# Key maxima as two float32r parts made on GpSimd, value buffers by first freed, and a new order table, in a phi-attention and cosine-FFN kernel

## The chip, the cores and the metric

The kernel runs on one core of one Trainium2 chip. The metric is the device time of one execution in microseconds (us). Three runs of the kernel before gave 1011.79, 1012.16 and 1014.1 us: a median of 1012.16 us.

Engine names in the rows: PE is TensorE, DVE is VectorE, ACT is ScalarE, POOL is GpSimd, SP is SyncE, which issues nearly all DMAs.

## The reference, cut to what matters

```python
def phi(x):                                   # x: q or k, 8 x 8 heads, 576 tokens of 64
    proj = einsum('bhsd,df->bhsf', x, w_phi)  # 128 features
    proj = proj - max(abs(proj), axis=-1)     # one maximum per token
    return concatenate([exp(proj), exp(-proj)], axis=-1)
q_p, k_p = phi(q), phi(k)
kv = einsum('bhsf,bhsd->bhfd', k_p, v);  z = sum(k_p over tokens)
x = (q_p @ kv) / (q_p @ z + 1e-06)            # 4608 tokens of 512
h = x @ w_in                                  # 512 -> 2048
out = (h * cos(h)) @ w_out                    # 2048 -> 512
```

## The kernel before

**Attention.** The 64 heads are worked in 32 units of two heads. For each unit one DMA brings q and k (`qk`), another the values with a column of ones (`vs`, two buffers that units take in turn). TensorE projects q (L572, L575) and k (`k_mm`, L618, and `k_end`, L643, for the last tokens). VectorE reduces each projected key to its absolute maximum (`k_max`, L656, tile `mk`), ScalarE takes the exponentials (`exp_k`, L673 and L676), TensorE forms `kv` (`kv_mm`, L722 and L728) and then the output (`x_mm`, L755 and L761). On the side of q the maximum goes over VectorE, three small GpSimd copies (`q_spread`, L603), a VectorE transposition (`q_turn`, L607) and four GpSimd subtractions (`q_sub`, L611).

In the first seven units (`K_SUMS`) the maximum of each key is subtracted by TensorE: `k_sub` (L664) multiplies a constant matrix `minus` (-1 on its diagonal) with `mk` spread over 128 columns and adds into the PSUM bank that holds the projection. Both operands are float32, so that the program runs each such product as two matmul records. There are 14 of these steps (units 0 to 6, two banks each; the short third part and all later units give the maximum to ScalarE as a bias instead). ScalarE can then take the exponential of a whole bank in one instruction for each sign (L673).

**FFN.** Weights arrive as 64-bit words, are converted into float32r pairs (high and low part) and stored; some are summed (`fold`: loaded as `f_raw` at L508, summed at L511 and L518, stored as `wo_sums`). 9 chunks of 512 tokens follow: the first three in 9 plain visits beside the attention (first product L974, second L1023 to L1025), then the other six, two at a time, in three fast visits (`visit_two`; first product at L1201 in steps of six matmuls that the planner calls `wide`, second product at L1374 to L1376). Float32r operands are multiplied as high x high, high x low and low x high. Before each fast visit x is loaded into four `x_raw` buffers (L1116) and split; the weights of the second product go through three `wo` buffers, loaded at L1351 (from `wo_parts`) or L1347 (from `wo_sums`).

**Order.** The program is a list of 3852 steps, each with its engine, cost, dependences and buffers. `ORDER` is a table written out by hand with the number of each step in program order; `plan()` walks it and every engine gets its instructions in that order, so that an instruction that waits holds everything behind it on its engine, and a DMA that waits for a buffer holds every later DMA of the SP queue. PSUM banks go to whichever was used last the longest ago in the table; the two value buffers alternate.

Of the kernel before, what the change touches and what calls it, by code (L numbers as in the profile page):

```python
# [26 lines left out]
def phi_attention_then_cos_ffn(ctx: ExitStack, tc: tile.TileContext, qkT, vS, w_phi, w_in, w_out, out, out_t):  # L27
# [41 lines left out]
    class Step:  # L69
# [190 lines left out]
    def plan():  # L260
        place = {steps[x]: i for i, x in enumerate(ORDER)}
        owner = [None] * len(banks)
        n_v = 0

        def last(b):
            return -1 if b is None else max(place[v] for v in b.users)
# [1327 lines left out]
```

## Time and profile before

| | us |
|---|---|
| median of three runs | 1012.16 |
| profiled execution, whole time | 1013.98 |
| profiled execution, first to last instruction (span) | 1012.3 |
| PE busy, share of the span | 991.7, 98% |
| DVE busy | 892.5, 88% |
| ACT busy | 769.7, 76% |
| POOL busy | 164.3, 16% |
| DMA, mean | 208 GB/s |

An engine is busy from an instruction's start to its end; matmul ends are modelled and matmuls overlap, so the distance between the starts of two matmuls says how long one holds the engine, not its duration. The granted TensorE clock is a share of 2.4 GHz; over the whole execution it was 0.998.

### The profile page before, as it was taken

What the parts mean: (1) busy time and instruction counts of PE and PEld (TensorE: products, weight loads), DVE (VectorE), ACT (ScalarE), POOL (GpSimd) and SP (SyncE); (2) the same over time, 40 slices, a digit from 0 to 9 for tenths busy, and PEclk for the clock granted to TensorE, in tenths of its full rate; (3) what the DMA queues carried; (4) which work ended last, traced back from release to release, by engine and by line L of the source; (5) the groups of instructions that cost most, each with busy time, mean ns of one, the idle gap of its engine ahead of it and who ended that gap; (6) DMA issues with size and microseconds to landing.
All of it is one profiled execution on the core that took longest, in us unless ns stands there. A gap on an engine that the chain in (4) does not pass through costs nothing.

```text
span 1012.3 us, 22252 instructions
## 1 busy us (share of the span) xinstructions
PE 991.7 (98%) x8586; PEld 803.5 (79%) x8586; DVE 892.5 (88%) x1590; ACT 769.7 (76%) x1575; POOL 164.3 (16%) x231
## 2 busy tenths in 40 slices
PE   9999999999999999999989999899999999999997
PEld 6778878888788878788767888688888888888886
DVE  6999999999899999899989979798778998787984
ACT  6899999688878988899997666557565766665653
POOL 4544130121112123333550000000000000000000
PEclk9999999999999999999999999999999999999999
DMA  6667776456676578888767663447546575375364
GB/s 233 187 192 229 240 214 206 138 188 233 208 236 205 212 227 286 282 283 254 232 198 247 222 217 141 158 165 270 200 151 228 171 219 206 126 247 203 98 225 145
DMA packets 104569, 210.60 MB, mean 208 GB/s; under 512 B 21392, under 2 KB 52240, under 8 KB 100880
## 3 DMA queue, kind: packets, MB, share of 16 engines
q1 hardware_dynamic: 104320, 209.13, 62.4%
q8 instruction: 67, 1.10, 0.4%
q14 instruction: 38, 0.31, 0.1%
q10 hardware_dynamic: 144, 0.07, 0.0%
HBM read 152.54 MB, written 56.62 MB: 207 GB/s over the span
## 4 chain that ended last, share of the span: by engine, by line
PE 77%; DVE 10%; DMA 7%; ACT 2%; issue 2%; POOL 1%; SPq 1%; DVEq 0%; POOLq 0%; ACTq 0%
PE bank L1201 23%; PE bank L974 9%; PE bank L1374 7%; PE bank L1376 7%; PE bank L1375 7%; PE bank L1023 3%; PE bank L1025 3%; PE bank L1024 3%; PE bank L755 3%; PE bank L722 3%; PE bank L618 2%; PE bank L572 2%; DMA vs<-vS 1%; DVE mk L656 1%; DVE m L589 1%
## 5 line engine op out<-in xcount | busy, mean ns | idle before, releaser
L1374 PE MATMUL bank<-gh,wo 128*128 128x512 f32 x336 | 132.4, 394 | 6.0 <-DMA wo<-wo_parts 4.2
L676 ACT ACTIVATE ek<-bank,mk 128x128 f32<-128x128 f32 x464 | 132.9, 486 | 4.2 <-DVE mk L659 2.3
L611 POOL TENSOR_TENSOR pq<-pq,bq 128x288 f32<-128x288 f32 x128 | 120.1, 969 | 97.9 <-DVE bq L607 72.0
L1376 PE MATMUL bank<-gl,wo 128*128 128x512 f32 x336 | 132.0, 393 | 0.0
L1375 PE MATMUL bank<-gh,wo 128*128 128x512 f32 x336 | 131.7, 392 | 0.0
L682 ACT ACTIVATE eq<-pq 128x576 f32<-128x576 f32 x128 | 83.8, 793 | 6.2 <-POOL pq L611 4.8
L603 POOL COPY m<-m 32x36 f32<-32x36 f32 x96 | 43.4, 452 | 268.3 <-DVE m L598 254.2
L1298 ACT ACTIVATE g<-hs 128x512 int32<-128x512 f32 x96 | 59.6, 626 | 34.7 <-DVE hs L1217 33.6
L1304 ACT ACTIVATE g<-g,halfpi 128x512 f32<-128x512 f32 x96 | 66.9, 717 | 24.8 <-DVE g L1301 24.6
L1201 PE MATMUL bank<-x_eq,wi 128*128 128x512 f32 x216 | 84.8, 393 | 0.1
L1211 ACT ACTIVATE hs<-bank 128x512 f32<-128x512 f32 x96 | 56.0, 591 | 35.6 <-PE bank L1201 25.2
L1374 PEld LDWEIGHTS bank<-gh,wo 128*128 128x128 f32 x336 | 63.4, 189 | 21.5 <-issue 6.7
L1023 PE MATMUL bank<-wo,gh 128*128 128x512 f32 x192 | 77.2, 402 | 0.6 <-ACT pq L583 0.4
L1201 PE MATMUL bank<-xh_t,wi 128*128 128x512 f32 x192 | 76.0, 396 | 0.3 <-ACT hs L1211 0.3
L1025 PE MATMUL bank<-wo,gl 128*128 128x512 f32 x192 | 75.3, 392 | 0.3 <-DVE gl L55 0.2
L1024 PE MATMUL bank<-wo,gh 128*128 128x512 f32 x192 | 74.9, 390 | 0.0
L1376 PEld LDWEIGHTS bank<-gl,wo 128*128 128x128 f32 x336 | 63.5, 189 | 14.2
L1301 DVE SCALAR_TENSOR_TENSOR g<-g,hs 128x512 f32<-128x512 int32 x96 | 64.9, 686 | 11.1 <-ACT g L1298 10.8
L1375 PEld LDWEIGHTS bank<-gh,wo 128*128 128x128 f32 x336 | 63.6, 189 | 13.8
L755 PEld LDWEIGHTS bank<-kv,eq 128*64 128x64 f32 x2048 | 64.9, 138 | 11.8 <-issue 3.4
L755 PE MATMUL bank<-kv,eq 128*64 128x65 f32 x2048 | 70.8, 223 | 1.3 <-DVE rb L781 0.5
L722 PE MATMUL bank<-vs,ek 128*64 128x65 f32 x2048 | 67.4, 223 | 1.9 <-ACT ek L676 1.5
(170 smaller groups left out, 2517.2 us busy)
## 6 DMA issues: line engine op xcount, KB each, us to landing
wi<-wi_parts SPq DMA_DIRECT2D x18, 1792.0 KB, 7.6
wo<-wo_sums SPq DMA_DIRECT2D x20, 1024.0 KB, 6.1
qk<-qkT SPq DMA_DIRECT2D x31, 640.0 KB, 5.3
x_raw<-xs SPq DMA_DIRECT2D x47, 256.0 KB, 4.0
wo<-wo_parts SPq DMA_DIRECT2D x22, 512.0 KB, 8.8
vs<-vS SPq DMA_DIRECT2D x32, 325.0 KB, 4.9
wi_raw<-w_in SPq DMA_DIRECT2D x8, 1024.0 KB, 6.3
wo_raw<-w_out SPq DMA_DIRECT2D x8, 1024.0 KB, 6.6
```

The costliest lines, as they stand in the source:

```text
L611: qeng.tensor_tensor(out=d["pq"][:, c], in0=d["pq"][:, c], in1=d["bq"][:, c], op=ALU.subtract)
L676: ACT.activation(out=e[:, g, s * P:(s + 1) * P], in_=pk[:, g, :], func=AF.Exp, scale=1.0 - 2.0 * s, bias=d["lk" if s == 0 else "mk", i][:, ...
L722: PE.matmul(out=acc[c:c + 64, n, i, :], lhsT=e[:, s, P * n + c:P * n + c + 64], rhs=vs[b["v"].slot][:, 2 * s + i, :], start=(s == 0 and i ...
L755: PE.matmul(out=ps[64 * h:64 * h + 64, 65 * t:65 * t + 65], lhsT=d["eq", i][:, n, c:c + 64], rhs=d["kv"][:, 2 * n + i, :], start=h not in ...
L974: PE.matmul(out=bank(b), lhsT=w[:, part, 2 * r + kt // 2, kt % 2 * P:(kt % 2 + 1) * P], rhs=d.get(("from", kt), d)[x, kt], start=(k == 0), ...
L1023: PE.matmul(out=a, lhsT=gh[:, t], rhs=w[:, 0, r], start=first, stop=False)
L1024: PE.matmul(out=a, lhsT=gh[:, t], rhs=w[:, 1, r], start=False, stop=False)
L1025: PE.matmul(out=a, lhsT=gl[:, t], rhs=w[:, 0, r], start=False, stop=last)
L1201: PE.matmul(out=bank(bank_b), lhsT=w[:, part, block, j * P:(j + 1) * P], rhs=d[x, name, j], start=start and k == 0, stop=k == 5, skip_grou ...
L1374: PE.matmul(out=a, lhsT=w_of(0, m), rhs=n["gh"], start=first, stop=False, skip_group_check=True)
L1375: PE.matmul(out=a, lhsT=w_of(1, m), rhs=n["gh"], start=False, stop=False, skip_group_check=True)
L1376: PE.matmul(out=a, lhsT=w_of(0, m), rhs=n["gl"], start=False, stop=True, skip_group_check=True)
```

## The change

1. `mk` is split on GpSimd: a new step `k_split` before each of the 14 `k_sub` steps makes a float32r high part (`tensor_scalar`) and a low part (`tensor_tensor`), each of 128 partitions x 4 elements. `k_sub` then runs two float32r products in place of one float32 product. `minus` becomes float32r, made from a float32 tile by one more GpSimd instruction at the start.
2. A value buffer is chosen as PSUM banks are: the one whose last use in the table is the earliest.
3. The table is a new one of 3866 numbers (14 steps more, so every later number shifts). Counted on PE with the new steps left out, 592 of 785 steps stand at another place, by up to 24 places; on SP 370 of 411, by up to 116.

What the new table does at the places that the prediction speaks of, counted from the two tables:

- Between the place of a `k_max` and that of the `k_sub` that uses it lie 3 to 8 PE steps, 5.3 on the mean of the 14 (before 1 to 6, 3.7 on the mean); about half of them are the short `k_end`, `q_end` and `k_sub`. On POOL, up to four `q_sub` steps and a `q_spread` stand near a `k_split`.
- In the old table all `x_mm` steps come before the first `wide` step. In the new one five `wide` steps stand before the last `x_mm` (of unit 31), and the summing of the last two `wo_parts` blocks comes later.
- The weights for the last two pairs of the first fast visit (the third load at L1351, two DMAs): in the old table they are queued on SP behind an `x_raw` load whose buffer VectorE frees while PE is one step of six matmuls ahead of the first use. In the new table six such steps lie between the last of the releases (of the `wo` buffer, and of the `x_raw` buffer queued ahead) and the first use.
- The weights for the first half of the last product (L1347): four steps of six matmuls between release and first use in the old table, six in the new one.

```diff
-        0, 3, 42, 4, 5, 59, 7, 45, 44, 1, 6, 8, 9, 17, 18, 10, 19, 46, 21, 11, 48, 58, 1265, 47, 12, 62, 14, 23, 20, 22, 15, 2, 49, 25,
...
+        0, 3, 5, 44, 4, 7, 60, 6, 8, 9, 62, 10, 1, 46, 65, 48, 63, 17, 11, 19, 22, 18, 20, 64, 12, 47, 70, 61, 49, 25, 68, 66, 23, 1279,
...
-        n_v = 0
+        owner_v = [None] * len(vs)
...
                 elif b.ring == "v":
-                    b.slot, n_v = n_v, 1 - n_v
+                    b.slot = min(range(len(vs)), key=lambda i: last(owner_v[i]))
+                    assert last(owner_v[b.slot]) < place[x]
+                    owner_v[b.slot] = b
...
-    minus = const.tile([P, P], F32, name="minus")
-    POOL.memset(minus, -1.0)
-    POOL.affine_select(out=minus, in_=minus, pattern=[[-1, P]], compare_op=ALU.is_equal, fill=0.0, base=0,
+    minus = const.tile([P, P], F32R, name="minus")
+    ones = const.tile([P, P], F32, name="ones")
+    POOL.memset(ones, -1.0)
+    POOL.affine_select(out=ones, in_=ones, pattern=[[-1, P]], compare_op=ALU.is_equal, fill=0.0, base=0,
                        channel_multiplier=1)
+    hi_of(POOL, minus, ones)
...
+        def k_split(i):
+            n = NSLOT if i < 2 else 1
+            parts = d["hk", i] = new("pk" if i < 2 else "pk_t", [P, n, 2], F32R, "hk", "hpk" if i < 2 else "hpk_t")
+            hi_of(POOL, parts[:, :, 0], d["mk", i])
+            lo_of(POOL, parts[:, :, 1], d["mk", i], parts[:, :, 0])
+
         def k_sub(i):
             n = NSLOT if i < 2 else 1
             pv = d["pk", i] = d["kps", i][:, 0:P * n].rearrange("p (g f) -> p g f", f=P)
-            PE.matmul(out=pv, lhsT=minus, rhs=d["mk", i].unsqueeze(2).broadcast_to([P, n, P]), start=False, stop=True,
-                      skip_group_check=True)
+            for k in range(2):
+                PE.matmul(out=pv, lhsT=minus, rhs=d["hk", i][:, :, k].unsqueeze(2).broadcast_to([P, n, P]), start=False, stop=k == 1,
+                          skip_group_check=True)
...
-                kms[i] = Step("PE", 0.86, lambda i=i: k_sub(i), [kms[i]], use=[kb[i], pks[i]], kind="a.k_sub")
+                kms[i] = Step("POOL", 0.3, lambda i=i: k_split(i), [kms[i]], use=[pks[i]], port=True, kind="a.k_split")
+                kms[i] = Step("PE", 0.46, lambda i=i: k_sub(i), [kms[i]], use=[kb[i], pks[i]], kind="a.k_sub")
```

`hi_of` on GpSimd is `tensor_scalar(out, in, 1.0, 0.0, mult, add)`, `lo_of` is `tensor_tensor(out, in, hi, subtract)`.

## Rows read from the trace of the kernel before

**Rows 1.** Page, part 1: busy time and instructions of each engine.
```profile
PE 991.7 (98%) x8586; PEld 803.5 (79%) x8586; DVE 892.5 (88%) x1590; ACT 769.7 (76%) x1575; POOL 164.3 (16%) x231
```

**Rows 2.** Windows, busy us by stretch: span, PE, PEld, DVE, ACT, POOL, clock, DMA, GB/s.
```profile
0.00:75.00 75.00, 73.14 (x1214) 55.58 (x1216) 65.51 (x138) 60.63 (x133) 36.48 (x57) 1.00 0.64 206
75.00:400.00 325.00, 324.22 (x3159) 266.36 (x3154) 304.48 (x532) 285.43 (x584) 70.64 (x94) 1.00 0.66 216
400.00:475.00 75.00, 72.60 (x1003) 58.53 (x1003) 69.47 (x147) 67.89 (x179) 28.14 (x38) 1.00 0.82 267
475.00:540.00 65.00, 59.51 (x1229) 48.64 (x1228) 60.34 (x139) 61.22 (x175) 29.02 (x44) 1.00 0.73 225
...
630.00:645.00 15.00, 10.78 (x41) 8.31 (x40) 10.07 (x17) 8.37 (x16) 0.00 (x0) 0.89 0.52 175
645.00:990.00 345.00, 344.98 (x1499) 280.75 (x1498) 293.18 (x472) 216.03 (x376) 0.00 (x0) 1.00 0.57 190
990.00:1012.00 22.00, 16.81 (x74) 13.30 (x72) 9.46 (x15) 7.29 (x12) 0.00 (x0) 1.00 0.35 127
```

**Rows 3.** Lines by shape, L1374 and k_max: count, busy us, mean ns, idle before.
```profile
L1374 PE MATMUL bank<-gh,wo 128*128 128x512 f32 x336 | 132.4, 394 | 6.0 <-DMA wo<-wo_parts 4.2 <-DMA wo<-wo_sums 1.7
...
L656 DVE TENSOR_REDUCE mk<-bank 128x4 f32<-128x512 f32 x64 | 42.6, 672 | 0.5 <-PE bank L618 0.3
```

**Rows 4.** Chain of waits, 600 to 1012 us: start, us, what.
```profile
626.11 1.39 PE bank L1201 x6
...
633.84 6.04 DMA wo<-wo_parts
...
640.02 0.47 PE bank L1374
...
642.35 0.43 PE bank L1374
...
644.36 0.23 PE bank L1376
...
990.28 6.99 DMA wo<-wo_sums
```

**Rows 5.** Timeline of the SP queue: start, us with its wait, line, DMA.
```profile
612.26 2.49 SPq L1351 DMA_DIRECT2D wo<-wo_parts  x4
615.09 18.65 SPq L1116 DMA_DIRECT2D x_raw<-xs  x2
633.84 1.18 SPq L1351 DMA_DIRECT2D wo<-wo_parts  x2
```

**Rows 6.** The tile mk: durations of k_sub's records, ns min/median/max.
```profile
L664 PE MATMUL bank<-mk,minus x28: 592/592/697, 10.5 to 63.7; 128*128 128x512 f32 x28
```

**Rows 7.** Timeline of all engines, 42 to 44 us: start, us, engine, line.
```profile
42.39 2.21 POOL L603 COPY m<-m 32x36 f32<-32x36 f32 x3 [1.10 <-DVE m L598]
...
42.69 1.02 PE L664 MATMUL bank<-mk,minus 128*128 128x512 f32 x2
...
43.36 1.16 DVE L398 SCALAR_TENSOR_TENSOR wo_t<-wo_raw,wo_t 128x1024 uint32<-128x1024 uint32 x1
```

**Rows 8.** Chain of waits, 255 to 266 us: a stretch of L974.
```profile
259.07 5.44 PE bank L974 x24
```

**Rows 9.** Lines L603 and L611 on POOL: durations, ns min/median/max.
```profile
L603 POOL COPY m<-m x96: 206/210/2384, 9.1 to 525.4; 32x36 f32<-32x36 f32 x96
...
L611 POOL TENSOR_TENSOR pq<-pq,bq x128: 791/808/1842, 11.8 to 530.0; 128x288 f32<-128x288 f32 x128
```

**Rows 10.** DMA issues by line: count, KB each, median us to landing.
```profile
wo<-wo_sums SPq DMA_DIRECT2D x20, 1024.0 KB, 6.1
...
wo<-wo_parts SPq DMA_DIRECT2D x22, 512.0 KB, 8.8
f_raw<-wo_parts SPq DMA_DIRECT2D x8, 1024.0 KB, 6.5
```

**Rows 11.** Waits of the SP queue, value loads: us in total, times, longest.
```profile
SPq L558 <- PE bank L728: 17.1, 6, 5.5
```

335 rows, old and new, of the table ORDER are left out of this document.

## The prediction

> **What bounds the kernel now.** I read the page's busy times first [rows 1]: PE works 98% of the span, DVE 88%, ACT 76%, POOL 16%. PE is the bound, but an average hides where another engine sets the pace, so the windows come next [rows 2]. The reader is to see four kinds of stretch. From 75 to 400 us and from 645 to 990 us PE has no visible idle time (0.8 and 0.0 us): there only fewer or cheaper matmuls help. From 0 to 75 us PE idles 1.9 us, while DVE is busy 65.5 of 75. From 400 to 540 us, the last attention units, PE idles 2.4 + 5.5 us, and in the second part DVE (60.3 of 65) and ACT (61.2 of 65) are busier than PE (59.5): the units' chain over three engines sets the end there. From 630 to 645 us and after 990 us PE idles 4.2 and 5.2 us; the lines view says what ended most of that [rows 3]: DMAs into `wo`, 4.2 us of `wo_parts` and 1.7 us of `wo_sums`. The chain of waits [rows 4] shows both places, at 633.84 and 990.28 us, and the timeline of the SP queue [rows 5] why the first is late: an `x_raw` load issued from 615.09 us on waited and held SP for 18.65 us with its neighbour; the weights behind it left only at 633.84 and landed 6.04 us later. They were late by their place in the queue, not by a slow transfer.
>
> **The change part by part.** The sum is made against the profiled execution, 1013.98 us (its span of 1012.3 and 1.7 around it); the median of the runs is 1.8 us below that.
>
> *The products of `k_sub`.* One record takes 592 ns and the two of one step together 1.02 us [rows 6, 7], so the second starts 0.43 us after the first and a step holds PE for 2 x 0.43 = 0.86 us. A float32r matmul of 128x512 in L974 holds it for 5.44 / 24 = 0.227 us [rows 8]; the new step has two, 0.45 us. Removed: 14 x 0.41 = 5.7 us, all before 75 us. No row shows a float32r product with its moving operand spread from one column; the float32 one runs at the plain rate, so I take 0.227. If it ran as slowly as the old pair, a step would hold PE for 4 x 0.43 and 14 steps would cost 12 us more.
>
> *The splits.* 28 small instructions on POOL, each of 4 elements on 128 partitions. Nearest row: the copies of 32x36, median 210 ns [rows 9]; a step is then 0.42 us, 14 are 5.9 us on an engine that is busy 36.5 of the first 75 us [rows 2]. No work of POOL's is on the bound. What matters is the wait put into the chain `k_max` - `k_split` - `k_sub`: `k_max` takes 0.67 us [rows 3], the split 0.42, together 1.1 us. Between the two places in the new table stand 5.3 PE steps on the mean. A step of the first 75 us holds PE 0.9 us on the mean (73.14 us over the 82 steps there, [rows 2]), half of those in question are short ones; I call the cover about 3 us, an estimate, and some 1.7 at the tightest. So the plain split is hidden. It is not when POOL is held: the slowest copy took 2.384 us [rows 9], and the three at 42.39 took 2.21 us together while DVE ran an instruction with two SBUF inputs [rows 7]. Behind a waiting `k_split` stand the `q_sub` steps and with them ACT's exponentials of q; behind a waiting `k_sub` all of PE. Bounds: nothing, if the cover holds everywhere; 14 x (0.67 + 2.38 + 0.21 - 3) = 3.6 us, if each split meets the slowest copy. On the side below nothing, the new table has at most the 1.9 us of PE's idle time in this stretch to give back. I take +1.5, since some splits are also queued behind `q_sub` steps (808 ns each, [rows 9]) and DVE, at 65.5 of 75, becomes the next limit once PE has 5.7 us less to do. The one POOL instruction for `minus` falls into the wait for the first loads: nothing.
>
> The Trainium skill ("SBUF — State Buffer", section "Who interferes with whom") states that a DVE instruction with two SBUF inputs and a GpSimd instruction that reads SBUF lock each other out for a whole instruction. It speaks against this change, since `k_split` reads SBUF twice while DVE converts weights with two-input instructions; the slow copies at 42.39 agree. By the rule each of the 28 could wait for one; that is the third rival below.
>
> *The first blocked load.* In the new table six steps of six matmuls lie between the last release and the first use of these weights. Such a step of L1201 takes 1.39 us [rows 4], so there are 8.3 us, against 6.04 us from issue to landing; before it was one step, 1.4 us. The stall should go: 4.2 us of idle time [rows 3], and what followed it. After the stall the granted clock of the window is 0.89 [rows 2], and matmuls stand 0.43 us apart, not 0.23 [rows 4]: that is the lower of the two clock levels, after an idle PE. From 640.02 to 644.36 run 12 matmuls, 4.34 - 12 x 0.23 = 1.6 us late. Together -5.8 us. What is late next: the same kind of load takes 8.8 us at the median when issued amid others [rows 10]; then 0.5 us would remain.
>
> *The last load.* Before, four steps (5.5 us) against 6.99 us to landing [rows 4]: 1.7 us of stall [rows 3]. In the new table six steps, 8.3 us, against 6.99 or the median of 6.1 [rows 10]: gone, -1.7.
>
> *The overlap at the end of attention.* Five `wide` steps, 5 x 1.39 = 6.95 us of PE work, now stand inside the stretch where PE idles 5.5 us in 65. They need the split x earlier and four more copies from PSUM on ACT, which is itself busy 61.2 of 65. Bounds: -5.5 (all of the idle time is filled) and +3 (ACT and DVE, already fuller than PE, get the chain of the last units 5% later). I take -3. The later summing lets `f_raw` loads arrive late (6.5 us, [rows 10]) on a DVE that has more room after 540 us: nothing.
>
> *Value buffers.* The waits of value loads for `kv_mm` are at most 5.5 us each and 17.1 in all [rows 11], on SP; a better choice can only move them, and PE shows no idle time behind most: 0, with -1 to +1 as bounds.
>
> *All else in the table.* Nearly every step has another neighbour. From 75 to 400 us there is 0.8 us of idle time to win; a single new blocked transfer costs up to 5.8. I take 0 and keep -1 to +6 for the range.
>
> Sum: 1013.98 - 5.7 + 1.5 - 5.8 - 1.7 - 3 = 999.3 us against the profiled execution, 997.5 against the median. I forecast 998.5.
>
> **The rivals.** (A) The weights come in time but the front gains nothing: DVE and ACT, not PE, set the pace up to 540 us. For: their shares after 475 us, DVE's 65.5 of 75 at the start. Against: PE has almost no idle time from 75 to 400 us, so a front that starts earlier stays earlier. Time: 1013.98 - 7.5 = 1006.5.
>
> (B) `k_sub` gains, but the new table only moves the blocked transfers: another load stands behind one that waits. For: SP still has one queue, with 370 of 411 steps at other places. Against: the two known stalls get 8.3 us of cover. Time: 1013.98 - 5.7 = 1008.3.
>
> (C) Slower: GpSimd, held by DVE. Place: the 14 `k_split` in the first 75 us. Price: each of the two instructions waits for one DVE instruction of 1.16 us as at 43.36 [rows 7], so 2 x (1.16 + 0.21) = 2.7 us, with 0.67 for `k_max` and one or two `q_sub` ahead (0.8 to 1.8 us each, [rows 9]) 4.2 to 5.2 us against about 3 of cover: 1.5 us late, 14 times, 21 us. It decides from 16.2 / 14 = 1.2 us late per step, where it eats all that the other terms win (16.2 us). Time: 1013.98 - 16.2 + 21 = 1018.8. Against it: the median copy is 210 ns and only few were held.
>
> (D) More than I count: the idle time of 400 to 540 us goes wholly (7.9 us, not 3) with the rest as in the sum and no loss in front: 1013.98 - 5.7 - 5.8 - 1.7 - 7.9 = 992.9.
>
> (E) The change doesn't do what it says, as the float32r product of a spread column is as slow as the old pair: 998.5 + 5.7 + 12 = 1016.
>
> **How the numbers follow.** Forecast 48%, with its own range 994 to 1003 (the bounds of the splits, the overlap and one small new wait); A 17%, B 13%, D 10%, C 6%, E 2%; 4% for a loss elsewhere in the table that cancels the gain, near 1012. About 0.3%, 3 us, is what a measurement of this kernel can tell from no change: faster is below 1009.1 us, slower above 1015.2. Faster: the forecast, A, D and two thirds of B, 84%. Same: the rest of B, the 4% and small parts of C and E, 10%. Slower: 6%. The range 992 to 1008.5 leaves out C, E, the cancelled case and the edges of B and D.
>
> **What would show it.** Right: `k_sub` records 0.23 us apart and 28 POOL instructions near 0.2 us; PE's starts of the first fast visit some 8 us earlier; no idle time of L1374 behind `wo` DMAs; no half-clock stretch after 600 us; PE idle below 5 us between 400 and 540 us. Wrong: PE waiting for `k_split` by over 1 us a step, PE idle time over 4 us before 75 us, or a new gap behind a DMA in the fast visits.

## The result and the profile after

The changed kernel takes 1000.43 us (median of 4 runs, 999.44 to 1000.98) against 1011.97 us before (4 runs, 1010.2 to 1014.1): a ratio of 0.9884, 95% interval [0.9863, 0.9905]. That is 1.9 us above the forecast, inside the forecast's own range. The profiled execution took 1000.19 us with a span of 998.4.

Lines of the changed kernel: `k_sub` is L676, `k_split` L52 (high part) and L55 (low part), `k_max` L661, `q_sub` L616, the `mm1` products L987, the first of the fast products on `wo` L1387. The page's busy times and the windows, in the stretches and columns of [rows 1, 2]:

```profile
PE 985.3 (99%) x8586; PEld 802.2 (80%) x8586; DVE 890.4 (89%) x1590; ACT 771.7 (77%) x1575; POOL 173.3 (17%) x260
```

```profile
0.00:75.00 75.00, 73.16 (x1260) 58.61 (x1262) 64.85 (x137) 61.23 (x132) 42.43 (x86) 1.00 0.68 220
75.00:400.00 325.00, 321.83 (x3085) 262.59 (x3080) 303.44 (x525) 284.31 (x583) 73.64 (x91) 1.00 0.65 213
400.00:475.00 75.00, 74.57 (x1103) 61.84 (x1100) 71.98 (x158) 71.04 (x186) 25.09 (x39) 1.00 0.88 295
475.00:540.00 65.00, 61.23 (x1178) 49.54 (x1177) 61.68 (x138) 62.39 (x175) 32.17 (x46) 1.00 0.69 213
...
630.00:645.00 15.00, 15.00 (x67) 12.36 (x66) 14.24 (x24) 10.69 (x20) 0.00 (x0) 1.00 0.69 222
```

The reader is to see where PE's idle time went. From 630 to 645 us it was 4.2 us and is none, and the granted clock is 1.00, not 0.89. From 400 to 540 us it was 2.4 + 5.5 us and is 0.4 + 3.8. From 75 to 400 us it rose, from 0.8 to 3.2 us. In the first 75 us nothing seems to have changed: PE is as busy as before, though its subtractions now hold it for 7.65 us and not for 12.8 (28 records each, from the start of each to PE's next start). The lines by shape say the same of the loads (count, busy us, mean ns, idle time before and what ended it, against [rows 3]); the 6.0 us behind `wo` are gone:

```profile
L1387 PE MATMUL bank<-gh,wo 128*128 128x512 f32 x336 | 131.5, 391 | 0.2 <-DVE o_t L1461 0.2
```

The tile `hk` of the changed kernel, the answer to [rows 6] (ns min/median/max), has the new records, and no instruction of a split above 0.52 us. From the start of a record to the next start on PE it is 0.21 to 0.32 us, so a step holds PE for 0.55 us on the mean (forecast 0.45):

```profile
L676 PE MATMUL bank<-hk,minus x28: 379/379/483, 10.1 to 60.8; 128*128 128x512 f32 x28
L52 POOL TENSOR_SCALAR hk<-mk x14: 185/195/203, 9.5 to 58.9; 128x4 fp32r<-128x4 f32 x14
L55 POOL TENSOR_TENSOR hk<-mk,hk x14: 203/205/517, 9.8 to 59.1; 128x4 fp32r<-128x4 f32 x14
```

A single row measures the pace of the front: where the first `mm1` product starts, behind 81 PE steps before and behind the same but one (`k_end` of unit 8, 0.2 us) after. The two numbers at the end of "first and last start" belong to the products of `xh_b`; first the kernel before, then the changed one:

```profile
L974 PE MATMUL bank<-xh_b,wi x192: 387/389/526, 71.6 to 445.5; 128*128 128x512 f32 x192
```

```profile
L987 PE MATMUL bank<-xh_b,wi x192: 387/389/504, 69.7 to 444.5; 128*128 128x512 f32 x192
```

Of 5.2 us less work on PE ahead of that product (12.8 - 7.65) 1.9 us show, and by the last one 1.0. A single row of this kind is weak: two kernels below that differ only by splits whose results nobody reads start this product 2.0 us apart, the one with more work first.

### The profile page after: what moved, and what is told of

The parts are those of the page before. It is cut to its first block, busy times and chain, and to the rows that moved or that the text cites. A ratio compares the mean times of both kernels' runs of the same rounds, so it can differ in the third digit from the quotient of the medians.

```text
span 998.4 us, 22304 instructions
## 1 busy us (share of the span) xinstructions
PE 985.3 (99%) x8586; PEld 802.2 (80%) x8586; DVE 890.4 (89%) x1590; ACT 771.7 (77%) x1575; POOL 173.3 (17%) x260
## 4 chain that ended last, share of the span: by engine, by line
PE 77%; DVE 9%; ACT 7%; DMA 4%; issue 2%; SPq 1%; POOL 0%; DVEq 0%; ACTq 0%; POOLq 0%
PE bank L1214 23%; PE bank L1389 8%; PE bank L1387 8%; PE bank L1388 8%; PE bank L987 7%; PE bank L735 4%; PE bank L768 4%; PE bank L1036 3%; PE bank L1038 2%; PE bank L1037 2%; PE bank L577 2%; PE bank L623 2%; ACT ek L688 2%; DMA wi_raw<-w_in 1%; PE bank L741 1%
## 5 line engine op out<-in xcount | busy, mean ns | idle before, releaser
L616 POOL TENSOR_TENSOR pq<-pq,bq 128x288 f32<-128x288 f32 x128 | 123.4, 993 | 94.5 <-DVE bq L612 72.4
L1387 PE MATMUL bank<-gh,wo 128*128 128x512 f32 x336 | 131.5, 391 | 0.2 <-DVE o_t L1461 0.2
L688 ACT ACTIVATE ek<-bank,mk 128x128 f32<-128x128 f32 x464 | 130.1, 443 | 0.5 <-DVE mk L664 0.3
L1317 ACT ACTIVATE g<-g,halfpi 128x512 f32<-128x512 f32 x96 | 67.1, 716 | 18.6 <-DVE g L1314 18.1
L1387 PEld LDWEIGHTS bank<-gh,wo 128*128 128x128 f32 x336 | 63.0, 188 | 14.1 <-DVE o_t L1461 0.6
L1230 DVE TENSOR_TENSOR hs<-bank,hs 128x512 f32<-128x512 f32 x72 | 49.1, 686 | 25.2 <-PE bank L1214 19.5
```

The costliest lines, as they stand in the source:

```text
L616: qeng.tensor_tensor(out=d["pq"][:, c], in0=d["pq"][:, c], in1=d["bq"][:, c], op=ALU.subtract)
L688: ACT.activation(out=e[:, g, s * P:(s + 1) * P], in_=pk[:, g, :], func=AF.Exp, scale=1.0 - 2.0 * s, bias=d["lk" if s == 0 else "mk", i][:, ...
L1387: PE.matmul(out=a, lhsT=w_of(0, m), rhs=n["gh"], start=first, stop=False, skip_group_check=True)
```

## Experiments

The times of a group stand beside runs of the kernel before on the same chip: medians of 1011.78, 1011.43, 1011.31 and 1012.21 us. Ratios are against those. Differences below about 2 us between kernels of different groups are read with care. Steps are named as in the order table, with unit and part: `k_split.u2.1`.

### The change taken apart: which part gives what

**The split alone, in the old table.**

```diff
 # ORDER of the kernel before, for each part of units 0 to 6
  k_max.u0.0,
+ k_split.u0.0,
# k_sub: two float32r products, as in the changed kernel
```

> The old order table with only the new subtraction in it: each split step of GpSimd stands right behind the max step it needs, the value buffers alternate as before, nothing else is moved. Theory A (the stretch up to 75 us and the tables behind it are bound by TensorE, so shorter subtractions count in full): the kernel before less about 5 us, 1006 to 1008 us. Theory B (the pace there is set by VectorE and ScalarE, and what TensorE saves comes back as short waits): 1 to 2 us less than before, 1010 to 1011 us.

Measured: 1019.04 us (10 runs, 1016.87 to 1021.74), ratio 1.0068 [1.0044, 1.0091]. Neither theory: it is 7.3 us slower than before. GpSimd's waits in the first 75 us of its trace (us in total, times, longest) and a piece of its timeline show what changed there; the single row between the two is of the changed kernel:

```profile
POOL hk L52 <- DVE mk L664: 14.9, 5, 8.5
...
POOL pq L619 <- ACT ek L688: 4.3, 2, 2.8
```

```profile
9.51 0.20 POOL L52 TENSOR_SCALAR hk<-mk 128x4 fp32r<-128x4 f32 x1 [7.71 <-DVE mk L661]
```

```profile
58.04 1.79 POOL L611 COPY m<-m 32x36 f32<-32x36 f32 x3 [1.99 <-DVE m L606]
62.19 0.19 POOL L52 TENSOR_SCALAR hk<-mk 128x4 fp32r<-128x4 f32 x1 [2.36 <-DVE mk L664]
62.47 0.20 POOL L55 TENSOR_TENSOR hk<-mk,hk 128x4 fp32r<-128x4 f32 x1
62.62 1.57 POOL L619 TENSOR_TENSOR pq<-pq,bq 128x288 f32<-128x288 f32 x2
65.31 1.02 POOL L52 TENSOR_SCALAR hk<-mk 128x4 fp32r<-128x4 f32 x1 [1.12 <-DVE mk L664]
66.42 0.20 POOL L55 TENSOR_TENSOR hk<-mk,hk 128x4 fp32r<-128x4 f32 x1
66.57 2.00 POOL L619 TENSOR_TENSOR pq<-pq,bq 128x288 f32<-128x288 f32 x2
```

GpSimd came to the split before VectorE had the maximum, and the `q_sub` steps (L619) stood behind it. Of the 14.9 us, 8.5 are the wait for the program's first maximum, which the changed kernel has too (7.71 us); the other four waits come to 6.4 us. From 0 to 70 us PE was busy 61.59 us, against 68.14 in the same window of the kernel before, and behind that the clock fell (window 70 to 80 us of this run):

```profile
70.00:80.00 10.00, 8.80 (x128) 6.62 (x130) 7.29 (x14) 7.67 (x22) 5.70 (x6) 0.66 0.59 199
```

A mean of 0.66 between the levels 1.0 and 0.5 means 6.8 of 10 us at the lower one (1.2 GHz), at most 3.4 us of work. This trace is that of the shortest of the ten runs: their granted clock has a median of 0.9925, that of the kernel before 0.998, a difference worth at most 5.6 us of work over 1019 us. The first `mm1` product starts at 82.1 us here, not at 71.6.

**The new table without the split.**

```diff
-            for k in range(2):
-                PE.matmul(out=pv, lhsT=minus, rhs=d["hk", i][:, :, k] ...
+            PE.matmul(out=pv, lhsT=minus, rhs=d["mk", i] ...      # float32, as before
-            k_split(i)
```

> The new table and the new value buffers, but the maxima subtracted by one float32 product as before, without the split. Theory A: the changed kernel (1000.4) and about 5 us more, 1005 to 1006 us, and the subtraction steps hold TensorE 0.86 us and more again. Theory B: 1 to 2 us more, 1001.5 to 1002.5 us, because TensorE had waited for the other engines there anyway.

Measured: 1003.11 us (6 runs, 1001.96 to 1004.11), ratio 0.9915 [0.9884, 0.9947]. So the table gives 8.7 us, and the split with its products 2.7 more, near theory B; the runs of this kernel and of the changed one don't overlap, though the intervals of their ratios do. The products of `xh_b`, first and last start:

```profile
L984 PE MATMUL bank<-xh_b,wi x192: 387/389/501, 74.1 to 447.7; 128*128 128x512 f32 x192
```

The first starts 2.5 us later than before the change, so in this trace the new table by itself is the worse one for the front. With the table held, the new subtraction takes 5.5 us off PE (13.2 - 7.65); of these 4.4 are there at the first `mm1` product (74.1 to 69.7) and 3.2 at the last (447.7 to 444.5). From 75 to 400 us PE idles 2.0 us here and 3.2 in the changed kernel: part of what the front won is handed back behind it.

**The blocked load alone.**

```diff
 # SP's order in the kernel before
+ r.load2#2   (third group of wo_parts, L1351), right behind n.mm2#9
  x_raw load
- r.load2#2
```

> The kernel before with one step moved: the third load of the output weights is issued from SP's queue ahead of the x_raw load that it stood behind. Theory A (the stall at 636 to 644 us is that load's place in the queue): the 4.2 us of idle time and the 1.6 us at half clock behind it both go, 5 to 6 us less than before, 1006 to 1007 us, and the granted clock of 630 to 645 us is 1.00. Rival: the stall moves to the x_raw load or to the next load of output weights, and the time stays within 1 us of before, 1011 to 1013 us.

Measured: 1005.23 us (9 runs, 1002.93 to 1010.03), ratio 0.994 [0.9913, 0.9967]: 6.5 us less than before, theory A, 0.8 us below its range. The window 630 to 645 us and the line by shape of this run:

```profile
630.00:645.00 15.00, 15.00 (x67) 12.32 (x67) 14.72 (x25) 10.86 (x19) 0.00 (x0) 1.00 0.43 145
```

```profile
L1379 PE MATMUL bank<-gh,wo 128*128 128x512 f32 x336 | 132.3, 394 | 2.0 <-DMA wo<-wo_sums 1.9
```

The 4.2 us behind `wo_parts` and the half-clock stretch are gone together, by moving one step of one queue; the 1.9 us behind `wo_sums` at the end stay, as the last load was left where it was. Not all of the difference between the two traces is this load: after 300 of the 2016 matmuls of the fast visits this kernel is 4.0 us ahead already (PE idles 0.1 us from 400 to 475 us, not 2.4, with the same steps there), after 600 it is 10.1 us ahead. The load's own part in the traces is 6.1 us.

**The overlap taken back.**

```diff
 # ORDER of the changed kernel, behind the last attention product
- n.wide#0, n.wide#7, n.wide#1, n.snap#0, n.wide#4, n.wide#2, n.even#0, n.snap#2   (among units 30, 31)
  x_mm.u31.0,
+ n.wide#0, n.wide#7, n.wide#1, n.snap#0, times.u29.1, n.wide#4, n.wide#2, n.even#0, n.snap#2,
```

> The changed kernel with its first five block products of the next stage, and the three steps that read them first, put behind the last attention product (x_mm of unit 31) as in the old table; one division step of unit 29 goes with them, because its bank is needed. Theory A (these five steps fill TensorE's waits for the last exponentials): 3 to 5.5 us more than the changed kernel, 1003.5 to 1006 us, and the idle time comes back at 510 to 540 us. Rival (the waits are for VectorE and ScalarE work that has to be done anyway, and only stand elsewhere): 1000 to 1001.5 us.

Measured: 1004.53 us (9 runs, 1001.08 to 1005.96), ratio 0.9927 [0.9903, 0.9951], 4.1 us more than the changed kernel. The window 475 to 540 us:

```profile
475.00:540.00 65.00, 58.91 (x1167) 48.11 (x1167) 58.92 (x136) 59.60 (x171) 32.22 (x46) 1.00 0.65 210
```

PE is busy 58.91 us, not 61.23: the five products did fill idle time, and PE idles here as before the change. Theory A. These are 2.3 us of the 4.1; from 540 to 630 us another 0.7 of idle time come back (89.31 us busy, not 90.00). The last 1.1 are spread over the stretches before, where nothing was moved.

The value buffers were not tried alone: in the new table the old rule, strict alternation, meets a buffer that is still in use at four units, so the new rule is what allows this table. The last load was not tried alone either; its price is read from the lines, 1.7 us before the change and 1.9 in the run above.

### What bounds the front

**Dead splits.** If the split lost time in the old table by GpSimd's queue, it must lose it even where nobody reads the result.

```diff
 k_split(i)                                   # stays, result unused
-rhs=d["hk", i][:, :, k]   (two products)
+rhs=d["mk", i]            (one float32 product)
```

> The old table with the early splits, whose results are not used: the maxima are subtracted by one float32 product straight from VectorE's result, as before. TensorE never waits for GpSimd here. Theory A (the loss of the old table with early splits comes by GpSimd's queue, behind which the spread products are late): as slow as with the splits used or slower, by the longer products, 1018 to 1025 us. Rival (the loss is the subtraction's own wait for its split): as fast as the kernel before, 1011 to 1013 us.

> The new table with the splits done and not used, and the float32 product of before. Set against the new table without splits (1003.1 us) it gives the splits' own price in the places where the new table has them. Theory A (they are covered there): 1002.5 to 1004 us. Theory B (they hold the spread products there too): 1004.5 us or more, so that the product by itself would be worth more than the 2.7 us by which the change differs from the table without splits.

Measured, old table: 1014.78 us (12 runs, 1012.7 to 1018.26), ratio 1.0037 [1.002, 1.0053]. New table: 1002.08 us (5 runs, 1001.65 to 1003.86), ratio 0.9908 [0.9891, 0.9926]. In the old table splits in the queue cost 3.4 of the 7.3 us, between the ranges of theory A and its rival. At the first `mm1` product their share is larger, 7.7 us of 10.5: it starts at 79.3 us here, at 82.1 with the splits used and at 71.6 before. What the used splits add: one wait of PE for a split, 2.5 us in the trace, and the lower clock (its median over the runs is 0.998 here, as before, and 0.9925 there). How the rest divides between the two is not shown. In the new table the unused splits cost nothing, theory A but for 0.4 us below its range; set against this run the used products are worth 1.7 us. Since nobody waits for an unused split, this does not price the subtraction's own wait; that is 0.7 us in the trace of the changed kernel. The products of `xh_b` here:

```profile
L984 PE MATMUL bank<-xh_b,wi x192: 387/389/504, 72.1 to 446.3; 128*128 128x512 f32 x192
```

**A later split in the old table.**

```diff
  k_max.u2.0,
- k_split.u2.0,
  ... (up to 12 steps, 6 or more left ahead of k_sub.u2.0)
+ k_split.u2.0,
```

> The old table with the new subtraction as in the run with the early splits (1019.0 us), but each split step stands up to 12 steps later behind its max, 6 or more steps ahead of its product, so that GpSimd seldom reaches it before VectorE has the maximum. Theory A (the early split stands first in GpSimd's queue, waits for the maximum, and holds the spread products queued behind it): most of the 7 us that the early split lost come back, 1008 to 1013 us, and GpSimd's waits for the maximum, 14.9 us there, fall under 5 us. Theory B (the hop through GpSimd and its extra work cost it, wherever they stand): 1017 to 1020 us.

Measured: 1014.33 us (12 runs, 1009.85 to 1017.53), ratio 1.0021 [1.0003, 1.0039]. 4.4 of the 7.3 us come back, between the two theories' ranges. GpSimd's wait for the maximum in a split, in the first 85 us, is 0.7 us and no more 14.9 (of which 8.5 at the start; a `q_spread` copy now waits there instead, 7.6 us):

```profile
POOL hk L52 <- DVE mk L664: 0.7, 3, 0.3
```

But it stays slower than the kernel without a split. So the place in the queue is worth more than the 2.9 us that are left. Whether the old table has a better place for the splits was not tried.

**Less work for TensorE, for VectorE, for both.** First the low product left out, then the maximum over half of the features, then both.

```diff
-            for k in range(2):
+            for k in range(1):
```

```diff
-            DVE.tensor_reduce(out=m, in_=pv, ...
+            DVE.tensor_reduce(out=m, in_=pv[:, :, 0:P // 2] if i in on_pe else pv, ...
```

> The changed kernel with the high part of the maxima alone subtracted: the product of the low parts is left out, which takes 14 times 0.22 us, 3.1 us, off TensorE in the first 75 us and changes what is computed by the low parts. Theory A (TensorE bounds that stretch): 3 us less than the changed kernel, 997 to 998 us. Theory B (VectorE and ScalarE set its pace, and what TensorE saves turns into waits): 999.5 to 1000.5 us.

> The changed kernel with the key maxima of the first units taken over half of the features only, which changes what is computed: 14 reductions of VectorE read 256 columns and not 512, by the ratio of the 128 and 512 column forms (0.28 and 0.66 us) about 0.25 us less each, 3.5 us in the first 75 us; TensorE's work is as it was. Theory A (VectorE, which is idle for hardly anything there, sets the pace of the front): 2 to 4 us less than the changed kernel, 996.5 to 998.5 us. Rival (TensorE bounds the front, and its small additions there have nothing to do with VectorE): 1000 to 1001 us.

> The half maxima and the one product together, so that VectorE has some 3.5 us and TensorE 3.1 us less to do in the front; both edits change what is computed. Theory A (VectorE sets the pace, TensorE is close behind it): more than either edit by itself, 994 to 997 us. If neither engine bounds the front but the chain from one unit to the next does, the time stays within 1 us of the changed kernel, 999.5 to 1001.5 us.

Measured: one product 1000.53 us (5 runs, 999.59 to 1001.83), ratio 0.9893 [0.9873, 0.9913]; half maxima 997.44 us (6 runs, 995.65 to 999.37), 0.9866 [0.9845, 0.9887]; both 1000.0 us (6 runs, 996.74 to 1004.11), 0.9893 [0.9866, 0.992]. The one product takes 2.8 us off PE (by the starts, 7.65 to 4.84) and brings nothing; the half maxima take 3.7 us off DVE (667 to 404 ns, 14 times) and bring 3.0. Windows from 15 to 75 us, in this order: the new table without the split, the changed kernel, one product.

```profile
15.00:75.00 60.00, 58.89 (x1104) 44.97 (x1101) 54.89 (x116) 51.53 (x114) 32.30 (x44) 1.00 0.61 199
```

```profile
15.00:75.00 60.00, 60.00 (x1154) 48.80 (x1150) 57.20 (x123) 53.84 (x119) 37.34 (x66) 1.00 0.66 205
```

```profile
15.00:75.00 60.00, 58.38 (x1112) 46.24 (x1110) 57.20 (x123) 53.52 (x117) 36.87 (x66) 1.00 0.64 201
```

With the float32 product DVE (third pair) does 54.9 us of work in these 60, with the two float32r products 57.2, and with one it does no more: 57.2 again, and the time saved appears as PE idle time, 1.6 us. (57.2 is no ceiling of VectorE's: in the old table, before the change, it did 57.77 here.) PE's 60.00 in the changed kernel looks like a bound, but less work on PE did not shorten the time; matmul ends are modelled, so that a short stall can be hidden in it. The first `mm1` product starts at 69.6 us with one product (69.7 in the changed kernel) and at 68.0 with half maxima:

```profile
L987 PE MATMUL bank<-xh_b,wi x192: 387/389/504, 69.6 to 444.3; 128*128 128x512 f32 x192
```

```profile
L987 PE MATMUL bank<-xh_b,wi x192: 387/389/500, 68.0 to 442.2; 128*128 128x512 f32 x192
```

Theory A for the half maxima, theory B for the one product. The kernel with both does not fit theory A: 994 to 997 us lie below its interval (997.8 to 1003.2 us against its group's 1011.31), and its median is that of the other theory, a chain from unit to unit. It spreads over 7 us, and its two longest runs, 1004.11 and 1002.11 us, are those with the lowest granted clock, 0.998 and 0.997; its profiled execution took 997.86 us and has the first and last of these products at 68.6 and 442.3 us, as with the half maxima alone. So in the trace VectorE's 3.7 us count again and PE's add nothing to them, but the times do not confirm the gain.

One rival is not ruled out. Half maxima also shorten each chain `k_max` - `k_split` - `k_sub` by 0.26 us, and no run here separates that from VectorE's load.

**A slower split.**

```diff
+            for _ in range(5):
+                hi_of(POOL, parts[:, :, 0], d["mk", i])
             lo_of(POOL, parts[:, :, 1], d["mk", i], parts[:, :, 0])
```

> The changed kernel with five more instructions of GpSimd in each split, about 1.0 to 1.4 us more from the maximum to the product, fourteen times. Theory A (the splits have about 3 us of cover where the new table puts them, 1.7 at the tightest): 0 to 2 us more than the changed kernel, 1000 to 1002.5 us. Rival (GpSimd's time reaches TensorE through the spread products behind the splits): 5 us or more, 1005 us and above.

Measured: 1016.62 us (6 runs, 1016.22 to 1018.49), ratio 1.0061 [1.0038, 1.0084]: 16.2 us more than the changed kernel: the rival's range, though not the rival's path. PE's waits in the first 90 us, GpSimd's timeline from 8 us on, and the windows to 75 us:

```profile
PE bank L678 <- POOL hk L52: 11.8, 6, 3.8
```

```profile
8.66 1.58 POOL L52 TENSOR_SCALAR hk<-mk 128x4 fp32r<-128x4 f32 x6 [6.86 <-DVE mk L661]
...
11.38 1.57 POOL L52 TENSOR_SCALAR hk<-mk 128x4 fp32r<-128x4 f32 x6
...
13.20 2.08 POOL L52 TENSOR_SCALAR hk<-mk 128x4 fp32r<-128x4 f32 x6
```

```profile
0.00:15.00 15.00, 9.50 (x64) 7.29 (x64) 7.45 (x15) 5.88 (x10) 5.82 (x30) 1.00 0.84 286
15.00:45.00 30.00, 25.29 (x414) 19.73 (x416) 20.18 (x42) 17.32 (x37) 21.44 (x56) 0.77 0.26 81
45.00:75.00 30.00, 26.86 (x452) 20.52 (x448) 24.88 (x50) 23.66 (x48) 21.03 (x56) 0.94 0.65 206
```

PE waits straight for the split, 11.8 us in 6 waits; 6.2 of them stand before 18.1 us, where the splits of units 0 and 1 follow one another on GpSimd and share one cover. Beside them is the clock: at a mean of 0.77 and 0.94 over 30 us each, at most 30 x 0.23 + 30 x 0.06 = 8.7 us of work are lost. Waits and clock together come to more than 16.2 us, so they can't simply be added.

### A version beyond the change

If VectorE sets the front's pace, a little less of its work should help, so a little of VectorE's work was given to ScalarE.

```diff
+            if u < 8:
+                ACT.activation(out=d["lk", i], in_=d["mk", i], func=AF.Copy, scale=-1.0)
+                return
             DVE.tensor_scalar(out=d["lk", i], in0=d["mk", i], scalar1=-1.0, ...
 # ORDER: each of these k_neg right ahead of its exp_k
```

> The changed kernel with the negated maxima of the first eight units made on ScalarE, each right before the exponential that reads it, and no more on VectorE. This takes ten instructions of 0.14 us, 1.4 us, off VectorE before 75 us and adds ten short ones to ScalarE, which has 1 to 2 us of room in each 15 us there. Theory A (VectorE sets the pace of the front, as the run with half maxima says): 0.5 to 1.4 us less than the changed kernel, 999 to 1000 us. Rival (ScalarE is as close to the bound, so that work only changes sides): 1000 to 1002 us.

Measured: 998.68 us (6 runs, 998.09 to 1002.07), ratio 0.9874 [0.9853, 0.9896]. That is 1.75 us below the changed kernel, on theory A's side and 0.3 us below its range, but runs and intervals overlap: faster than before the change for certain, faster than the change likely and not shown. In its trace (998.09 us) the products of `xh_b` start from 68.8 to 442.4 us, 0.9 and 2.1 us ahead of the changed kernel. This edit leaves the chain from a maximum to its subtraction as it was, so it speaks for VectorE's load rather than that chain, as far as one trace goes.

## Why the prediction was right, and where it was not

**The sum.** Measured against predicted, by the terms. The first load: 6.5 us (6.1 in the traces), predicted 5.8; mechanism and place as told, clock included. The last load: the 1.7 us were read from the line before [rows 3] and are gone. The overlap: 4.1 us, predicted 3. `k_sub` with its splits: 2.7 us, predicted 5.7 - 1.5 = 4.2. "All else in the table": taken as 0. The new table without splits gives 8.7 us where its three known gains come to 6.5 + 1.7 + 4.1 = 12.3, so all else costs some 3.6 us, inside the bounds of -1 to +6. That is an estimate from medians of several groups; in the traces 2.5 us are lost in the front (the first `mm1` product at 74.1 us, though at 72.1 with unused splits) and 1.2 from 75 to 400 us, where PE idles 2.0 us in that kernel and 0.8 before.

The traces before and after say the same by stretch. After 300 of the 2016 matmuls of the fast visits the changed kernel is 5.0 us ahead, after 600 it is 11.2, at the last one 13.8. So everything ahead of the fast visits' first load is worth 5.0 us, where the terms 5.7 - 1.5 + 3 say 7.2; the first load is worth 6.2 us, the rest 2.6.

The forecast came close by luck in part: two terms that were too good (by 1.5 and some 3.6 us) were partly paid for by two that were too small (by 0.7 and 1.1). Besides, 998.5 stands between the sum against the profiled execution (999.3) and the one against the median (997.5) without a reason; against the second, which is the sum for a median, the result is 2.9 us longer.

**The step that failed.** "Removed: 14 x 0.41 = 5.7 us, all before 75 us": the products were priced as PE time, in a stretch where the text itself had set DVE's 65.5 of 75 us beside PE's 1.9 us of idle time, and drew nothing from it but part of the 1.5 for the splits. PE's own saving is nearly as told, 5.2 us (5.5 with the table held), as a step holds PE for 0.92 and 0.55 us and not 0.86 and 0.45. But only 2.7 us of it reach the time (1.7 against the table with unused splits): some is lost in the front, some from 75 to 400 us. In the front PE's busy share of 98% was not the whole bound. The row that said so stood there: DVE at 65.5 of 75 us [rows 2], and it works almost without a gap once the first inputs are there. Rival A named VectorE for the front and was nearer there, but wrong in that nothing would be gained. The saving counts until DVE is nearly full (54.9 to 57.2 us of 60 in the new table), and not beyond, as the run with one product shows. That VectorE's load, and not the chain through it, is what limits is likely and not shown. The difference of 1.5 us between 4.2 and 2.7 is small by itself; the run with one product and the one with half maxima carry this reading.

**The splits' cover.** "About 3 us, some 1.7 at the tightest" was a mean over the steps. Where the table puts them the plain splits cost next to nothing: the unused ones hold up no queue, and PE waited for a used one once, 0.7 us. But there is little reserve: some 1.4 us more in each cost 16.2 us, since four splits share the first cover and the clock fell behind PE's waits. The bound of 3.6 us was far too low for a slow split, and it left the clock out. The third rival's price was nearer (21 us at 1.5 us a step), by another cause: the splits' own length, not VectorE's hold on GpSimd.

**The table as part of the subtraction's price.** The prediction counted the splits and the table as separate terms. They are not: the same split costs 7.3 us in the old table, all gains of the products included, and brings 2.7 in the new one.

**Signs told beforehand.** The records 0.2 us long on POOL, no idle time behind `wo`, no half clock after 600 us, 4.2 us of PE idle time from 400 to 540 us (below 5): all there. Two came in part: the records of `k_sub` stand 0.21 to 0.32 us apart, not 0.23 throughout, and the first fast visit runs 5.0 us earlier, not some 8, which is where the front's missing gain shows. None of the signs of being wrong is there: PE waited 0.7 us in all for the split, it idles 1.8 us before 75 us, and it has no gap behind a DMA in the fast visits.

## To carry to other kernels

Before a saving on the busiest engine is counted, look at each other engine in the same stretch: one that works almost without gaps can set the pace, even if the first is shown at 100% busy, and a run that takes work off one engine alone tells. An instruction put into an in-order queue is priced by what stands behind it and by whether its input is there when the queue arrives, not by its own 0.2 us; move it behind that time before you judge it. A stall behind a load is best followed to the load's issue: one step moved in one queue was worth 6.5 us here, more than the arithmetic.

## What the runs showed of the hardware

A lower granted clock followed TensorE's waits. In the slow split PE was idle for 5.5 of the first 15 us, and the clock's mean over the next 30 us was 0.77; in the early split PE was busy 61.6 of the first 70 us, with a last wait of 1.96 us up to 71.20 us, and the mean from 70 to 80 us was 0.66. In the changed kernel, with 73.2 of 75 us busy, it stayed at 1.00.

A GpSimd instruction on 4 elements took 1.19 us and not 0.20 when it met a VectorE instruction with two SBUF inputs, and ended with it (timeline of the early split in the old table):

```profile
43.10 1.23 DVE L55 TENSOR_TENSOR wi<-wi_t,wi 128x1024 fp32r<-128x1024 f32 x1
43.20 1.19 POOL L52 TENSOR_SCALAR hk<-mk 128x4 fp32r<-128x4 f32 x1
```

The Trainium skill ("SBUF — State Buffer", section "Who interferes with whom") says that such a pair locks each other out; this row agrees, at 44.33 and 44.39 us for the two ends. In the changed kernel only one of the 28 instructions took more than 0.21 us (0.52), so the rule cost it next to nothing. In the early split four of 28 took 0.64 to 1.19 us; such waits may be a part of what the splits cost in the old table, and no run here prices them apart.
